# Two token chunks share one Strassen down projection in a transformer block

## The chip, the cores and the metric

The kernel runs on one core of a Trainium2 chip. The metric is the device time of one execution in microseconds. Five engines work side by side: TensorE (PE) multiplies matrices, VectorE (DVE) and ScalarE (ACT) work element by element, GpSimd (POOL) issues some of the transfers and does a few sums, SyncE (SP) issues most transfers. A matmul here is one instruction that multiplies a 128x128 tile by a 128x512 tile and adds the product to a bank of 128x512 fp32 sums in PSUM, of which there are eight.

## The reference

One transformer block on 2048 tokens of width 1024, in bf16: a norm, a sliding attention of 32 heads in which every token looks at 8 tokens (itself and every second one before it), and a gated feed forward without a nonlinearity.

```python
x = A_x                                             # (1, 2048, 1024)
qkv = layernorm(x) @ wqkv                           # wqkv 1024 x 3072
idx = pos[:, None] - 2 * arange(8)[None, :]         # 8 keys a token, masked where idx < 0
logits = einsum("bhsd,bhswd->bhsw", q, k[idx]) * 32 ** -0.5
o = einsum("bhsw,bhswd->bhsd", softmax(logits), v[idx])
h = x + o @ wo                                      # wo 1024 x 1024
n = layernorm(h)
g, u = n @ w_gate, n @ w_up                         # 1024 x 3584 each
out = h + (g * u) @ w_down                          # w_down 3584 x 1024
```

## The kernel before

The tokens are cut into four chunks of 512 (0 to 3). TensorE's instructions stand in this order: q, k and v of all chunks; then for chunk 0 wo and norm, gate and up; wo of chunk 1; down of chunk 0; gate and up of chunk 1; then, interleaved, down of chunk 1 and wo of chunks 2 and 3; at the end chunks 2 and 3 together (the "pair stage": gate, up and down, all in Strassen's way, untouched by the change). Attention is VectorE's work and needs no matmul: it is a generator that hands out a piece at a time. The `Background` object issues such a piece after a group of matmuls, as long as its account of VectorE's time (`rate`, `credit`, `spend`) allows.

```python
    def attention(c):
        qD, kD = qkv_in["q", c], qkv_in["k", c]
        ...
            for j in range(2):
                nc.vector.tensor_tensor(prod[:, j], qD[:], kD[:, :, o:o + SUB], ALU.mult)   # 128x4096
                yield 2.3
        ...
        nc.vector.tensor_tensor(lg[:], lg[:], mx[...], ALU.subtract)
        nc.scalar.activation(lg[:], lg[:], ACTF.Exp, scale=float(DH) ** -0.5)
        yield 3.5
        ...
        nc.gpsimd.dma_start(od[c].rearrange("c g d s -> (c g) d s"), oD[:])
        oT = att.tile([128, KO, 4, SUB], BF, tag="oT", name=f"oT{c}")
        for cp in range(4):
            nc.gpsimd.dma_start(oT[:, :, cp, :], od[c][cp].rearrange(...))
```

The attention's result oD goes to DRAM and comes back transposed as oT, four slices, one for each 128 tokens. `wo_ln2` multiplies oT by wo, adds to the residual h and normalizes on VectorE:

```python
    def wo_ln2(c):
        for t in range(4):
            for hf in range(2):
                ...                                    # 8 matmuls
                nc.vector.tensor_tensor(hs[t][:, bass.ts(hf, 512)], ps[:], hs[t][:, bass.ts(hf, 512)], ALU.add)
                if hf == 1:
                    stats(hs[t], mv4, t)               # two BN_STATS, one aggregate, on VectorE
                    rstd_of(mv4, rs4, t, t + 1)
                elif t > 0:
                    norm(t - 1)
                bg.step(GROUP_US)
```

Gate and up of a chunk, and the down projection of chunk 0:

```python
    def ffn1(c, lnT, at={}):
        for b in range(7):
            for j in range(4):
                mm_group(pg, wts["wg", c, b], j, lnT)          # 8 matmuls
                nc.scalar.copy(gs[:], pg[:])
                bg.step(GROUP_US)
                mm_group(pu, wts["wu", c, b], j, lnT)          # 8 matmuls
                nc.scalar.copy(us[:], pu[:])
                nc.vector.tensor_tensor(gs[:], gs[:], us[:], ALU.mult)
                abs_sum(c, b, j)                               # ScalarE: sum of |w|, 128x1024
                bg.step(GROUP_US)
    def ffn2(c, hf, hT, hs, between={}):
        for b in range(4):
            for j in range(7):
                for t in range(4):
                    nc.tensor.matmul(acc[t][:], lhsT=hT[f][:, bass.ts(t, 128)], rhs=wts["wd", c, hf, b][:, j, :], ...)
                abs_sum_down(hf, b, j)                         # ScalarE: sum of |w|, 128x512
```

The sums of absolute values fix powers of two by which weights and h are scaled before they become fp16, the type in which Strassen's sums and differences are formed (`scale_gu` for gate and up, `scale_d` for down, `scale_h1` for h).

Chunk 1's down projection is one level of Strassen (in Winograd's form): seven products of half-sized blocks in place of eight. The four blocks of h are two halves of the tokens (256 each) by even and odd tiles of the inner dimension, those of w_down even and odd tiles by halves of the columns. `dprod` is one such product for 128 tokens (14 matmuls), and each runs for q = 0 and 1:

```python
    def dprod(ps, q, lhs, rhs, fresh, lo=0, n=TC):
        for k in range(NP):                                    # 14
            nc.tensor.matmul(ps[...], lhsT=lhs[k][:, bass.ts(q, 128)], rhs=rhs[k][...], ...)
    hT = ffn1(1, lnT2, {0: scale_d.rows, 2: scale_d.total, (6, 1): first_blocks})
    E1 = {"11": [t[:, 0:256] for t in hT[0::2]], "21": [t[:, 256:512] for t in hT[0::2]],
          "12": [t[:, 0:256] for t in hT[1::2]], "22": [t[:, 256:512] for t in hT[1::2]]}
```

Of the kernel before, what the change touches and what calls it, by code (L numbers as in the profile page):

```python
# [18 lines left out]
D = 1024  # L19
# [59 lines left out]
def kernel(  # L79
# [41 lines left out]

    bg = Background()
# [13 lines left out]
    def stream_wd(c, hf):  # L136
        for b in range(4):
            stream.append((("wd", c, hf, b), wd_v[:, bass.ts(b, 7), bass.ts(hf, 512)], 7))

    NH = NF // 4  # L140
    for c in range(2):
        stream_wo(c)
        if c > 0:
            stream_wd(0, 0)
            stream_wd(0, 1)
        for b in range(7):
            stream.append((("wg", c, b), wg_v[:, :, bass.ts(b, 512)], KO))
            stream.append((("wu", c, b), wu_v[:, :, bass.ts(b, 512)], KO))
    def stream_down(name, e, hf, halves):
        for a in halves:  # L150
            stream.append((("dn", name, a), wd_e[e][:, bass.ts(a, 7), bass.ts(hf, 512)], 7))

    stream_down("21", 1, 0, (0, 1))
    stream_down("11", 0, 0, (0, 1))
    stream_wo(2)
    stream_down("12", 0, 1, (0,))
# [100 lines left out]
    class NormOnScalar(Norm1):  # L257

        def sums(self):
            room = small.tile([128, 4, 4], F32, tag="nroom", name=f"nroom{self.c}")  # L260
            self.s, self.nm, self.ss, self.nb = (room[:, i, :] for i in range(4))
            junk = lnp.tile([128, D], BF, tag="ln", name=f"njunk{self.c}")
            xs = xtiles[self.c]
            for t in range(4):
                nc.scalar.activation(junk[:], xs[t][:], ACTF.Copy, accum_out=self.s[:, t:t + 1])
                yield "later", GROUP_US
            nc.scalar.activation(self.nm, self.s, ACTF.Copy, scale=-1.0 / D)
            for t in range(4):
                nc.scalar.activation(junk[:], xs[t][:], ACTF.Square, bias=self.nm[:, t:t + 1],
                                     accum_out=self.ss[:, t:t + 1])  # L270
                yield "later", GROUP_US
            nc.scalar.activation(self.rs4[:], self.ss, ACTF.Ln, bias=eps[:], scale=1.0 / D)
            nc.scalar.activation(self.rs4[:], self.rs4[:], ACTF.Exp, scale=-0.5)
            for t in range(4):
                nc.scalar.activation(self.nb[:, t:t + 1], self.nm[:, t:t + 1], ACTF.Copy, scale=self.rs4[:, t:t + 1])

        def rows(self):
            for t in range(4):
                ln = lnp.tile([128, D], BF, tag="ln", name=f"ln{self.c}_{t}")
                nc.scalar.activation(ln[:], xtiles[self.c][t][:], ACTF.Identity, bias=self.nb[:, t:t + 1],  # L280
                                     scale=self.rs4[:, t:t + 1])
                self.lns[t] = ln
                self.transpose(t)
                yield "later", GROUP_US
# [158 lines left out]

    def attention(c):
        qD, kD = qkv_in["q", c], qkv_in["k", c]
        lg = att.tile([128, W, SUB], F32, tag="lg", name=f"lg{c}")
        for wp in range(W // 2):
# [14 lines left out]
            yield 1.0  # L462
        if c == 0:
# [6 lines left out]
        nc.vector.tensor_tensor(lg[:], lg[:], mx[:, None, :].to_broadcast((128, W, SUB)), ALU.subtract)  # L470
        nc.scalar.activation(lg[:], lg[:], ACTF.Exp, scale=float(DH) ** -0.5)
# [9 lines left out]
        prefetch_qk(c + 1)  # L481
# [7 lines left out]
        for wp in range(W // 2):  # L489
# [7 lines left out]
            prefetch_qk(c + 1)  # L497
# [12 lines left out]
        oTs[c] = oT  # L510
        while c + 1 < NCH and ("q", c + 1) not in qkv_in:
# [7 lines left out]
    def wo_ln2(c):  # L519
# [8 lines left out]
        for t in range(4):  # L528
            for hf in range(2):
# [12 lines left out]
                bg.spend(0.7)  # L542
                bg.step(GROUP_US)
        norm(3)
        retire(2)
        return lnT, hs
# [35 lines left out]
    scale_gu, scale_d, scale_h = Scale("gu", 56), Scale("d", 56), Scale("h", 56)  # L582
    scale_h1 = Scale("h1", 28)

    def abs_sum(c, b, j):
        wt = wts["wg" if c == 0 else "wu", c, b]
        junk = lnp.tile([128, 2, 512], BF, tag="ln", name=f"junk{c}_{b}_{j}")
        scale_gu.add(28 * c + 4 * b + j, wt[:, bass.ts(j, 2), :], junk[:])

    def abs_sum_down(hf, b, j):  # L590
        junk = lnp.tile([128, 512], BF, tag="ln", name=f"junkd{hf}_{b}_{j}")
        scale_d.add(28 * hf + 7 * b + j, wts["wd", 0, hf, b][:, j, :], junk[:])
# [5 lines left out]
    def abs_sum_h1(f, ht):  # L598
        junk = lnp.tile([128, TC], BF, tag="ln", name=f"junke{f}")
        scale_h1.add(f, ht[:], junk[:])  # L600

    def ffn1(c, lnT, at={}):
        hT = []
        for b in range(7):
            if b == 5 and c + 1 < NCH:
                hss[c + 1] = load_x(c + 1, "h", nc.sync)
            for j in range(4):
                pg = psum.tile([128, TC], F32, tag="mm", name=f"pg{c}_{b}_{j}")
                mm_group(pg, wts["wg", c, b], j, lnT)
                gs = t1k.tile([128, TC], BF, tag="t1k", name=f"gs{c}_{b}_{j}")  # L610
                nc.scalar.copy(gs[:], pg[:])  # L611
                bg.step(GROUP_US)
                pu = psum.tile([128, TC], F32, tag="mm", name=f"pu{c}_{b}_{j}")
                mm_group(pu, wts["wu", c, b], j, lnT)
                us = t1k.tile([128, TC], BF, tag="t1k", name=f"us{c}_{b}_{j}")
                nc.scalar.copy(us[:], pu[:])  # L616
                nc.vector.tensor_tensor(gs[:], gs[:], us[:], ALU.mult)  # L617
                abs_sum(c, b, j)
                bg.spend(0.45)
                bg.step(GROUP_US)  # L620
                hT.append(gs)
                if (b, j) in at:
                    at[b, j]()
                f = len(hT) - 3
                if c == 1 and f >= 0:
                    abs_sum_h1(f, hT[f])
# [3 lines left out]
        if c == 1:  # L630
            for f in range(NF - 2, NF):
                abs_sum_h1(f, hT[f])
        return hT

    def ffn2_store(c, t, hf, acc, hs, lo=0, n=512):
        cols = bass.ds(hf * 512 + lo, n)
        nc.vector.tensor_tensor(hs[t][:, cols], acc[:], hs[t][:, cols], ALU.add)
        nc.sync.dma_start(outf[bass.ds(c * TC + t * 128, 128), cols], hs[t][:, cols])

    def ffn2(c, hf, hT, hs, between={}):  # L640
        acc = [psum.tile([128, 512], F32, tag="mm", name=f"acc{c}_{hf}_{t}") for t in range(4)]
        for b in range(4):
            for j in range(7):
                f = b * 7 + j
                for t in range(4):
                    nc.tensor.matmul(acc[t][:], lhsT=hT[f][:, bass.ts(t, 128)],  # L646
                                     rhs=wts["wd", c, hf, b][:, j, :],
                                     start=(f == 0), stop=(f == NF - 1))
                if c == 0:
                    abs_sum_down(hf, b, j)  # L650
                bg.step(0.86)
            retire()
            if b in between:
                between[b]()
        for t in range(4):
            ffn2_store(c, t, hf, acc[t], hs)
            bg.spend(0.7)


# [95 lines left out]
    pump(6)  # L755
    bg.add(norm1[3].sums(), bg.now + 18.0)
    start_attention(0)
    qkv(1, range(4))
# [11 lines left out]
    bg.rate = 0.98  # L770
# [3 lines left out]
    lnT2, hs = nxt  # L774
    hT = ffn1(0, lnT2)
    bg.finish(atts[1])
    nxt = wo_ln2(1)
    for hf in range(2):
        ffn2(0, hf, hT, hs)
    lnT2, hs = nxt  # L780
# [37 lines left out]
    dn = {}  # L818

    def first_blocks():  # L820
        dn["11"] = [wts["dn", "11", a] for a in range(2)]
        dn["21"] = [wts["dn", "21", a] for a in range(2)]
        conv_down(dn["11"])

    hT = ffn1(1, lnT2, {0: scale_d.rows, 2: scale_d.total, (6, 1): first_blocks})
    hs1 = hs
    E1 = {"11": [t[:, 0:256] for t in hT[0::2]], "21": [t[:, 256:512] for t in hT[0::2]],
          "12": [t[:, 0:256] for t in hT[1::2]], "22": [t[:, 256:512] for t in hT[1::2]]}
    EF = {k: [f16(a) for a in E1[k]] for k in E1}
    conv_down(dn["21"], nc.scalar)  # L830
    scale_gu.rows()
    scale_h1.rows()
    bg.finish(atts[2])
    ex = [psum.tile([128, TC], F32, tag="mm", name=f"ex{q}") for q in range(2)]
    ey = [psum.tile([128, TC], F32, tag="mm", name=f"ey{q}") for q in range(2)]
    for q in range(2):
        dprod(ex[q], q, E1["11"], fcells(dn["11"]), True)
        bg.step(3.0)

    h3 = att.tile([128, 4, D], BF, tag="qD", name="h3")  # L840
    nc.sync.dma_start(h3[:], x[bass.ts(3, TC), :].rearrange("(t p) d -> p t d", p=128))
    hss[3] = [h3[:, t, :] for t in range(4)]
# [3 lines left out]
    def wo_adds(c, at):  # L846
        hs = hss[c]
        for t in range(4):
            for hf in range(2):
# [5 lines left out]
                bg.spend(0.7)  # L855
                bg.step(GROUP_US)
# [133 lines left out]
    for t in range(4):  # L990
        ln_rows(3, t, l3)
# [166 lines left out]
```

## Time and profile before

| what | value |
|---|---|
| time, median of 3 runs | 777.28 us (776.94 to 777.30) |
| span of the profiled run | 775.2 us |
| granted TensorE clock | 1.000 |
| matmuls in the trace | 3691 |
| ScalarE busy | 484.0 us (62% of the span) |
| GpSimd busy | 142.1 us (18%) |
| wo of chunk 1 begins | 287.88 us |
| down of chunk 0 | 301.69 to 350.0 us |
| first matmul of the pair stage | 516.77 us |

Times of the profile are microseconds from the start of the span. A group of instructions is named by line, engine, operation and "output<-input" with the shapes, then comes the number of instructions, then busy time and mean duration in ns, then the idle time of the engine just before them with what ended it. The chain of waits follows the end of the program back, at each step to what released it. A row of the table by stage gives each engine's busy time within a stretch. Since a matmul's end is modelled, busy time of PE is not proof of work at full rate; the chain and the waits are.

### The profile page before, as it was taken

What the parts mean: (1) busy time and instruction counts of PE and PEld (TensorE: products, weight loads), DVE (VectorE), ACT (ScalarE), POOL (GpSimd) and SP (SyncE); (2) the same over time, 40 slices, a digit from 0 to 9 for tenths busy, and PEclk for the clock granted to TensorE, in tenths of its full rate; (3) what the DMA queues carried; (4) which work ended last, traced back from release to release, by engine and by line L of the source; (5) the groups of instructions that cost most, each with busy time, mean ns of one, the idle gap of its engine ahead of it and who ended that gap; (6) DMA issues with size and microseconds to landing.
All of it is one profiled execution on the core that took longest, in us unless ns stands there. A gap on an engine that the chain in (4) does not pass through costs nothing.

```text
span 775.2 us, 10420 instructions
## 1 busy us (share of the span) xinstructions
PE 769.3 (99%) x3691; PEld 353.5 (46%) x3691; DVE 605.3 (78%) x766; ACT 484.0 (62%) x1040; POOL 142.1 (18%) x152
## 2 busy tenths in 40 slices
PE   8999999999999999999999999999999999999998
PEld 6444444444444444444444444444444444444444
DVE  5639999999999989999979859985553444578863
ACT  4639564322866662965777899746677776788240
POOL 0000000200002000011000001008778687600000
PEclk9999999999999999999999999999999999999999
DMA  8998896997947964978445592644332423740001
GB/s 278 265 260 199 157 230 151 299 271 224 310 133 236 308 235 125 288 257 277 142 143 192 182 299 68 157 98 114 109 95 69 109 59 106 240 140 28 0 28 55
DMA packets 183716, 134.38 MB, mean 173 GB/s; under 512 B 81264, under 2 KB 176496, under 8 KB 181616
## 3 DMA queue, kind: packets, MB, share of 16 engines
q1 hardware_dynamic: 176912, 110.12, 50.9%
q0 software_dynamic: 3584, 22.02, 8.9%
q10 hardware_dynamic: 3168, 1.57, 0.8%
q8 instruction: 29, 0.48, 0.3%
q14 instruction: 23, 0.19, 0.1%
HBM read 104.86 MB, written 22.02 MB: 164 GB/s over the span
## 4 chain that ended last, share of the span: by engine, by line
PE 93%; DVE 3%; DMA 2%; ACT 1%; issue 0%; ACTq 0%; DVEq 0%
PE ps L411 20%; PE pg L411 12%; PE pu L411 12%; PE dx L807 6%; PE pz L700 6%; PE acc L646 6%; PE py L700 6%; PE px L700 6%; PE wo L532 4%; PE wo L852 4%; PE pv L700 3%; PE dy L807 3%; PE ex L807 2%; DMA lnT<-lnr 1%; DMA w_qkv<-in_A_wqkv_dram 1%; PE ps L372 1%
## 5 line engine op out<-in xcount | busy, mean ns | idle before, releaser
L411 PE MATMUL ps<-lnT,w_qkv 128*128 128x512 bf16 x736 | 159.5, 379 | 0.0
L411 PEld LDWEIGHTS <-w_qkv 128*128 128x128 bf16 x736 | 71.9, 98 | 86.2
L411 PE MATMUL pu<-lnT,w_wu 128*128 128x512 bf16 x448 | 105.8, 379 | 0.0
L411 PE MATMUL pg<-lnT,w_wg 128*128 128x512 bf16 x448 | 105.8, 379 | 0.0
L324 ACT CAST sg<-ps 128x512 bf16<-128x512 f32 x96 | 55.2, 585 | 52.3 <-PE ps L411 49.2
L451 DVE TENSOR_TENSOR prod<-qD,kD 128x4096 bf16<-128x4096 bf16 x32 | 72.4, 2285 | 12.8 <-DMA kD<-kd 12.7
L494 DVE TENSOR_TENSOR pv<-vD,at 128x4096 bf16<-128x4096 bf16 x32 | 72.5, 2285 | 0.3
L700 PEld LDWEIGHTS <-sw 128*128 128x128 f16 x448 | 43.8, 98 | 53.8 <-issue 1.2
L411 PEld LDWEIGHTS <-w_wu 128*128 128x128 bf16 x448 | 43.8, 98 | 52.9
L411 PEld LDWEIGHTS <-w_wg 128*128 128x128 bf16 x448 | 43.7, 98 | 52.8
L616 ACT CAST us<-pu 128x512 bf16<-128x512 f32 x56 | 33.0, 590 | 43.0 <-PE pu L411 41.8
L700 PE MATMUL px<-lnT,ws 128*128 128x512 bf16 x224 | 55.2, 379 | 0.0
L700 PEld LDWEIGHTS <-ws 128*128 128x128 f16 x336 | 32.9, 98 | 39.7
L506 POOL DMA_DIRECT2D od<-oD x4 | 2.2, 542 | 264.3 <-DVE oD L504 264.3
L646 PE MATMUL acc<-w_wd,gs 128*128 128x512 bf16 x224 | 48.5, 379 | 0.0
L681 POOL TENSOR_TENSOR sw<-ws 128x512 f16<-128x512 f16 x26 | 30.0, 1152 | 85.1 <-PE py L700 77.8
L611 ACT CAST gs<-pg 128x512 bf16<-128x512 f32 x56 | 32.6, 583 | 12.9 <-PE pg L411 10.6
L453 DVE TENSOR_TENSOR prod<-prod 128x4096 bf16<-128x4096 bf16 x16 | 36.6, 2289 | 0.4
L560 ACT ACTIVATE junkd<-w_wd 128x512 bf16<-128x512 bf16 x56 | 34.3, 613 | 0.0
L646 PEld LDWEIGHTS <-gs 128*128 128x128 bf16 x224 | 21.9, 98 | 26.4
L617 DVE TENSOR_TENSOR gs<-gs,us 128x512 bf16<-128x512 bf16 x56 | 23.5, 419 | 12.5 <-ACT us L616 12.5
L185 ACT ACTIVATE rs<-mv,eps 128x1 f32<-128x1 f32 (+1 forms) x21 | 6.2, 297 | 42.0 <-DVE mv L182 36.6
(321 smaller groups left out, 1391.5 us busy)
## 6 DMA issues: line engine op xcount, KB each, us to landing
w_wg<-in_B_w_gate_dram SPq DMA_DIRECT2D x14, 1024.0 KB, 6.7
w_wu<-in_B_w_up_dram SPq DMA_DIRECT2D x14, 1024.0 KB, 5.4
w_wd<-in_B_w_down_dram SPq DMA_DIRECT2D x8, 896.0 KB, 6.2
w_pair<-in_B_w_gate_dram SPq DMA_DIRECT2D x14, 512.0 KB, 4.0
w_pair<-in_B_w_up_dram SPq DMA_DIRECT2D x14, 512.0 KB, 5.2
w_wo<-in_A_wo_dram SPq DMA_DIRECT2D x6, 1024.0 KB, 6.2
w_qkv<-in_A_wqkv_dram SPq DMA_DIRECT2D x5, 1024.0 KB, 11.0
kd<-sg SPq DMA_DIRECT2D x32, 144.0 KB, 3.3
```

Source lines behind the costliest of these rows:

```text
L324: nc.scalar.copy(sg[:, HB:HB + TC], ps[:])
L411: nc.tensor.matmul(ps[:], lhsT=wt[:, ko, bass.ts(j, 128)], rhs=rhs[:, ko, :], start=(ko == 0), stop=(ko == KO - 1))
L451: nc.vector.tensor_tensor(prod[:, j], qD[:], kD[:, :, o:o + SUB], ALU.mult)
L453: nc.vector.tensor_tensor(prod[:, :, 0:16], prod[:, :, 0:16], prod[:, :, 16:32], ALU.add)
L494: nc.vector.tensor_tensor(pv[:, j], vD[:, :, o:o + SUB], at[:, w, None, :].to_broadcast((128, DH, SUB)), ALU.mult)
L532: nc.tensor.matmul(ps[:], lhsT=oTs[c][:, kk, t, :], rhs=wts["wo", c, hf][:, kk, :], start=(kk == 0), stop=(kk == KO - 1))
L560: nc.scalar.activation(junk, src, ACTF.Abs, accum_out=self.l1[:, k:k + 1])
L611: nc.scalar.copy(gs[:], pg[:])
L616: nc.scalar.copy(us[:], pu[:])
L646: nc.tensor.matmul(acc[t][:], lhsT=hT[f][:, bass.ts(t, 128)], rhs=wts["wd", c, hf, b][:, j, :], start=(f == 0), stop=(f == NF - 1))
L700: nc.tensor.matmul(ps[:], lhsT=lhs[:, ko, :], rhs=rhs[:, ko, :], start=(fresh and ko == 0), stop=(ko == 3), skip_group_check=not fresh)
L807: nc.tensor.matmul(ps[:, bass.ds(lo, n)], lhsT=lhs[k][:, bass.ts(q, 128)], rhs=rhs[k][:, bass.ds(lo, n)], start=(fresh and k == 0), stop=( ...
```

## The change

The down projections of chunks 0 and 1 become one Strassen product: the rows of the left matrix are now the two chunks, so block A11 is chunk 0's even tiles of h, A12 its odd ones, A21 and A22 those of chunk 1, and each of the seven products runs for four row tiles of 128 tokens. It is meant to save matmuls: chunk 0's down projection was a standard one.

```diff
-    for hf in range(2):
-        ffn2(0, hf, hT, hs)
-    hT = ffn1(1, lnT2, {0: scale_d.rows, 2: scale_d.total, (6, 1): first_blocks})
-    for q in range(2):
-        dprod(ex[q], q, E1["11"], fcells(dn["11"]), True)
+    hT0 = ffn1_first(nxt[0], {(4, 2): wo_1})
+    bg.finish(norm2[1])
+    ffn1_second(norm2[0].lnT, {})
...
+    for q in range(4):
+        dprod(xs[q], q, A11, cells_of(b11, NH), True)
...
+    for q in range(4):
+        dprod(xs[q], q, A12, cells_of(b21, NH), False)
+        put(0, q, 0, hs0[q][:, 0:512], xs[q], 1.0, hs0[q][:, 0:512])
```

What stands around it has to change with it.

*Storage.* h of chunk 0 stays in SBUF (28 tiles), so h of chunk 1 no longer fits; it is made in a ring of three places, stored in DRAM and read back in blocks. Half of chunk 0's and all of chunk 1's residual rows go to DRAM and back, too.

```diff
+            nc.vector.tensor_tensor(g, g, u, ALU.mult)                 # 128x1024, two tiles of h at a time
+            nc.sync.dma_start(hd1[:, bass.ts(i, 2), :], g)
...
+    load_h1(a21, 0)
+    load_h1(a22, 1)                                                    # a22 is read a second time later
```

*wo of chunk 1* moves into the middle of chunk 0's gate and up (block 4, j = 2), and its norm goes to ScalarE, one step after each group of matmuls:

```diff
+    class Norm2(NormOnScalar):
+        pace = 0.9 * GROUP_US
+        def finish(self):
+            yield from self.devs()
+            yield from self.rows()
...
+    def wo_1():
+        bg.finish(sums)
+        bg.finish(atts[1])
+        n = wo_norm(1)
+        norm2.append(n.finish())
+        bg.add(norm2[1], bg.now, first=True)
```

*Sums of absolute values.* Gate and up are summed four row tiles at a time (128x2048), the gate's blocks 4 and 5 during chunk 1; of w_down, one half of the columns is read through a ring buffer during the q, k, v stage, the other half is summed from the Strassen blocks B11 and B21.

```diff
-        scale_gu.add(28 * c + 4 * b + j, wt[:, bass.ts(j, 2), :], junk[:])
+        scale_gu.add((14 if key == "wu" else 0) + 2 * b + i, wt[:, bass.ts(i, 4), :], junk)
+                if j % 2 and b not in (4, 5):
+                    abs_sum("wg", 0, b, j // 2, junk[:])
+    def abs_down():
+        for p in range(7):
+            scale_d.add(p, rows_of(p), rows_of(p))
+            if p + 2 < 7:
+                load(p + 2)
+            yield "later", 4.9 * GROUP_US
```

*The attention's place in the order.* A later attention waits until the one before has ended, the exp is issued a step later, chunk 3's q and k are loaded one step later, and the account of VectorE's time changes:

```diff
+        while c and c - 1 not in over:
+            yield "later", 1.0
+        yield "later", 4.0 if c == 0 else 1.5
         nc.scalar.activation(lg[:], lg[:], ACTF.Exp, scale=float(DH) ** -0.5)
-            prefetch_qk(c + 1)
+            if c != 2 or wp > 0:
+                prefetch_qk(c + 1)
-    bg.rate = 0.98
+    bg.rate = 1.03
+    bg.spend(8.0)
```

*The order of the products.* With B the blocks of w_down, S and T the sums of Strassen's form (S1 = A21 + A22, S2 = S1 - A11, S3 = A11 - A21 formed as A22 - S2, S4 = A12 - S2; T1 = B12 - B11, T2 = B22 - T1, T3 = B22 - B12, T4 = B21 - T2): wo of chunk 2, A11·B11, A12·B21, S1·T1, S2·T2, S4·B22, wo of chunk 3, S3·T3, A22·T4, then the pair stage as before. Each result is scaled back, added to the residual rows and stored by `put`.

## The prediction

> **What bounds the kernel now.** I read the page's busy line first, then the chain of waits, then TensorE's waits, and last a table of busy time by stage. The page says which engine has no room:
>
> ```profile
> PE 769.3 (99%) x3691; PEld 353.5 (46%) x3691; DVE 605.3 (78%) x766; ACT 484.0 (62%) x1040; POOL 142.1 (18%) x152
> PE 93%; DVE 3%; DMA 2%; ACT 1%; issue 0%; ACTq 0%; DVEq 0%
> ```
>
> Busy PE is modelled, so 99% alone proves little. The chain proves it: from 27 us to the pair stage its long pieces are all matmuls.
>
> ```profile
> 27.16 136.41 PE ps L411 x632
> 163.56 13.81 PE wo L532 x64
> ...
> 287.88 13.81 PE wo L532 x64
> 301.69 48.35 PE acc L646 x224
> 446.76 6.04 PE ex L807 x28
> 456.50 10.36 PE wo L852 x48
> ```
>
> Two things are read here. 48.35 us / 224 = 0.2159 us for one 128x512 matmul, back to back: the price of a matmul. And each piece starts where the one before ended: 287.88 + 13.81 = 301.69. Then TensorE's waits. Past 27 us there are two, both behind the last output additions of chunk 1:
>
> ```profile
> 519.08 1.02 PE L700 MATMUL pv<-prodx,sw 128*128 128x512 f16 x4 [0.41 <-DVE h L812]
> ...
> 521.19 1.02 PE L700 MATMUL pv<-prodx,sw 128*128 128x512 f16 x4 [0.22 <-DVE h L812]
> ```
>
> Together 0.63 us. So nothing can be gained but by fewer matmuls, by those 0.63 us, or in the first 27 us, which the change leaves alone. The stage table says who would take over (columns: window, then busy us of PE, PEld, DVE, ACT, POOL, each with its instructions; clock; DMA share; GB/s):
>
> ```profile
> 191.20:253.00 61.80, 61.80 (x288) 28.00 (x287) 60.19 (x50) 40.98 (x78) 4.62 (x6) 1.00 0.77 232
> 253.00:302.00 49.00, 49.00 (x229) 22.21 (x228) 45.17 (x56) 25.34 (x48) 1.07 (x2) 1.00 0.72 242
> 302.00:350.00 48.00, 48.00 (x224) 21.77 (x223) 46.85 (x33) 35.30 (x116) 3.12 (x4) 1.00 0.78 243
> 350.00:399.00 49.00, 49.00 (x230) 22.23 (x228) 43.40 (x53) 34.24 (x72) 1.51 (x3) 1.00 0.58 185
> 399.00:447.00 48.00, 48.00 (x224) 21.71 (x223) 43.72 (x36) 39.46 (x90) 0.56 (x1) 1.00 0.55 185
> ...
> 479.00:493.00 14.00, 14.00 (x66) 6.37 (x65) 14.00 (x38) 11.62 (x22) 0.00 (x0) 1.00 0.04 12
> ```
>
> VectorE is 89 to 100% busy in each of these. It is idle 22% of the span, but not in the stages that the change rewrites: 239.3 of 255.8 us from 191.2 to 447.
>
> **What the Trainium skill says.** "TensorE: Matmul & The Clock Gate", section "Wait — 56ns, not 53.3ns?", puts back-to-back 512-column matmuls at 215.7 ns start to start on a warm array; the trace's 215.9 agrees, and the clock is 1.00 in every row above. "VectorE: DVE Perf Modes", section "Why `tensor_tensor` can't do 2×_2P or 4×": two source tensors use up both read ports. That fits these rows: the sum of two tensors costs nearly twice the scaling of one of the same size.
>
> ```profile
> L494 DVE TENSOR_TENSOR pv<-vD,at 128x4096 bf16<-128x4096 bf16 x32 | 72.5, 2285 | 0.3
> L617 DVE TENSOR_TENSOR gs<-gs,us 128x512 bf16<-128x512 bf16 x56 | 23.5, 419 | 12.5 <-ACT us L616 12.5
> L800 DVE TENSOR_TENSOR kx<-w_dn,w_dn 128x3584 f16<-128x3584 f16 x2 | 4.0, 2014 | 0.0
> L788 DVE TENSOR_SCALAR w_dn<-w_dn,sbd 128x3584 f16<-128x3584 bf16 x3 | 3.4, 1148 | 0.2 <-issue 0.2
> ```
>
> "ScalarE: Activation LUTs", section "What ACT_TABLE_LOAD costs", gives an ACTIVATE with immediates 186 ns + 0.833 ns an element. For the new 2048-element sums this makes 1.89 us, an estimate; the 1024-element sums of before show 1067 ns, where the same formula gives 1039. "DMA: Bandwidth & Descriptors", section "Issuing engines are not separate DMA queues": loads issued by different engines share the same 16 DMA engines. The DMA shares of 0.55 to 0.78 above are therefore what the new reloads find occupied.
>
> **The change part by part.**
>
> *Matmuls.* Before, chunk 0's down projection is standard: 4 row tiles x 28 x 2 halves = 224. Chunk 1 has its own seven products: 7 x 2 x 14 = 196. After: one set of seven for both chunks, 7 x 4 x 14 = 392. 420 - 392 = 28 matmuls less; 28 x 0.2159 = 6.04 us. The projections, gate and up, wo, and chunks 2 and 3 keep theirs. TensorE without new waits gives 777.28 - 6.04 = 771.24, and 770.6 if the 0.63 us go as well. This is the floor.
>
> *The new timetable of TensorE*, in groups of 8 matmuls (1.73 us) from 191.2: gate and up of chunk 0 until blocks 0 to 3 and half of block 4 are done (36 groups: 253.35), wo of chunk 1 to 267.2 (before, from 287.88), the rest to 301.7, gate and up of chunk 1 to 398.4, wo of chunk 2 to 412.2. Then products of 56 matmuls, 12.09 us each: A11·B11 to 424.3, A12·B21 to 436.4, S1·T1 to 448.5, S2·T2 to 460.6, S4·B22 to 472.7; wo of chunk 3 to 486.5; S3·T3 to 498.6; A22·T4 to 510.7, where the pair stage begins (before at 516.77). Every part is judged by what must be ready at these times.
>
> *oT of chunk 1*, needed at 253.35, 34.5 us sooner than before. Before's GpSimd timeline:
>
> ```profile
> 236.17 0.54 POOL L506 DMA_DIRECT2D od<-oD  x1 [62.50 <-DVE oD L504]
> 245.09 3.54 POOL L509 DMA_DIRECT2D oT<-od  x4 [8.39 <-PE pg L411]
> ```
>
> The store took till 245.1 (the 8.39 us; the engine named had long been done), and the median landing of an oT slice is 4.8 us on the page. VectorE's order in front of oD hardly changes: I sum 44.6 us of work from 191.2, so oD is done near 235.9, as before. The first slice lands at 249 to 253 us and each later one is needed 3.45 us (two groups) after it. Cost: 0 to 1 us.
>
> *VectorE until the last gate product of chunk 1.* After's order, at the durations above (4096 elements 2.26 us, 512 elements 0.36, somewhat under the rows' means because neighbours overlap: an estimate): 44.6 us to oD of chunk 1, then 162.1: the rest of attention 2 and the larger part of 3 (some 140), 13 products of 1024 elements 8.2, 16 of 512 5.8, 8 additions of wo 5.0, with the small rest. 191.2 + 44.6 + 162.1 is about 398, and TensorE is at 398.4. No slack, but no deficit: chunk 1's norm went to ScalarE (8 BN of 0.68, 4 of 0.2, 4 rows of 0.55 = 8.4 us less) and the eight additions of chunk 0's output (8 x 0.68 = 5.4) are gone.
>
> *Sums for the pair on VectorE*, from 398: 40 us up to T1 = B12 - B11: rest of attention 3 13.6, wo additions 5, scaling of A21, A22, B11 and B12 about 7, S1 and T1 8, outputs 2.8. T1's second half is ready at 438 to 440; the eighth matmul of S1·T1 reads it first, at 436.4 + 7 x 0.216 = 437.9. Cost 0.3 to 2 us. T2 and S2 (2 x 1.97 + 14 x 0.35) are ready at 447.6 to 449.6 for 448.5: mostly hidden behind the former wait. A22·T4 adds into the banks of S3·T3, so each bank's output must be read first; by the same sum over after's order (additions of wo, statistics of chunk 3, T4, then the outputs) VectorE has read the first at about 499.3 against 498.6: 0.7 us.
>
> *ScalarE.* The row sums of gate and up become 28 of 1.9 us instead of 56 of 1.07 + 0.2, the down sums 23 instead of 56, sums of h grow from 28 to 42. In chunk 1's gate and up, two steps cost 4 x 0.48 + 1.9 + 1.05 = 4.9 us of TensorE's 6.9 (6.8 with an additional gate sum): hidden. The 16 sums over B11 and B21 cost 12 x 1.05 + 4 x 0.61 = 15 us from 403, done at 418.5 to 421; their total is wanted on TensorE at 421.3. No cost, or a few tenths.
>
> *Transfers.* New: h of chunk 1 out (14 x 256 KB) and A21, A22 and again A22 back, residual rows out and in. Those of 398 to 420 (B12's and B21's parts, A21, A22, some 6.4 MB) take 21 us at 300 GB/s, which the page's slices show to be reached: on land by 418 to 420, first needed from 413 to 423. No cost to 1 us.
>
> Sum: 771.24 - 0.63 + about 0.4 (oT) + 0.6 (T1) + 0.7 (output before A22·T4) = 772.3.
>
> **The rivals.** (a) VectorE takes over. For: it is 94% busy over the stretch and my sum ends on the very microsecond of TensorE's. Each exp also makes it wait for ScalarE, 1 to 3 us an attention, unless the added yield fills that. Against: the same engine carried 60.19 of 61.80 us in before without a single TensorE wait there. It would show as waits of 2 to 5 us before S1·T1 and S2·T2: 774 to 777. (b) A transfer is late: oT of chunk 1, A21 and A22, or wo of chunk 0, whose buffer now comes later because a ring for the down sums takes one. For: shares of 0.8 and landings of 8.2 us for one megabyte. Against: the median 4.8. 774 to 778. (c) Everything is hidden: 770.6 to 771.3. The order was plainly laid out against these deadlines (later q and k of chunk 3, wo of chunk 1 split from its norm), so I give (c) and my sum together 70%, (a) 20%, (b) 10%.
>
> **Range and chances.** Predicted 772.3. Low 770.4 is the floor less the spread of runs (0.36 us); high 775.5 holds the middle of (a). More than 2% faster would be below 761.7, which 28 matmuls can't give; more than 2% slower is above 792.8, which needs 22 us of new waits. Chances 0.01, 0.97, 0.02.
>
> **What would show it.** Right: TensorE 28 matmuls fewer; the pair stage beginning at 510.7 plus the waits; waits under 2 us, named after VectorE's T1 or an output. Wrong: a wait in front of wo of chunk 1 (oT step), in gate and up of chunk 1 (VectorE or buffers), at A11·B11 (transfers, total), or a tail after the pair stage's start longer than 258.4 us. The prediction fails if such waits sum above 4 us.

## The result and the profile after

| | before | after |
|---|---|---|
| time, median | 777.11 us (4 runs, 776.74 to 777.30) | 774.48 us (4 runs, 773.42 to 775.07) |
| ratio after to before, 95% interval | | 0.9965, 0.9948 to 0.9982 |
| span of the profiled run | 775.2 us | 772.1 us |
| matmuls in the trace | 3691 | 3663 |
| wo of chunk 1 begins | 287.88 us | 253.38 us |
| first matmul of the pair stage | 516.77 us | 514.63 us |

The changed kernel is 2.6 us faster. 5.0 were predicted, 6.0 are what the matmuls left out are worth. The page of the changed kernel, busy line and shares of the chain by engine:

```profile
PE 764.2 (99%) x3663; PEld 351.1 (45%) x3663; DVE 606.2 (79%) x718; ACT 513.4 (66%) x979; POOL 141.9 (18%) x152
PE 75%; DVE 15%; ACT 4%; issue 3%; DMA 3%; ACTq 0%; DVEq 0%; SPq 0%
```

28 matmuls are gone, as counted. The second line is new: before, 93% of the chain was TensorE; now VectorE carries 15%. That reads like a kernel bound by VectorE for 15% of its time, but it means something else: the chain is followed back from the end, and where it meets a wait of TensorE it steps to whoever ended that wait and walks back along that engine as long as it stays busy. One wait suffices to hand over a hundred microseconds. TensorE's timeline from A11·B11 to the pair stage has that wait (the bracket is idle time, and its releaser):

```profile
412.38 9.23 PE L944 MATMUL ex<-w_dn,gs 128*128 128x512 bf16 x42
424.49 0.38 PE L645 MATMUL ey<-rowbd,ones 128*128 128x512 bf16 x1 [2.88 <-DVE rowbd L640]
424.70 3.18 PE L944 MATMUL ex<-w_dn,gs 128*128 128x512 bf16 x14
428.07 12.25 PE L944 MATMUL ex<-w_dn,gs 128*128 128x512 bf16 x56 [0.18 <-ACT ey L1067]
440.15 12.25 PE L944 MATMUL ev<-w_dn,a 128*128 128x512 f16 x56
...
502.54 12.25 PE L944 MATMUL ez<-t,a22r 128*128 128x512 f16 x56
514.63 1.67 PE L826 MATMUL px<-lnT,ws 128*128 128x512 bf16 x7
```

Only these two waits of over 0.1 us stand in the whole span after the start. The single matmul `ey<-rowbd,ones` sums the absolute values of w_down over the partitions (the "total"); TensorE waits for `rowbd`, the row sums reduced on VectorE. Then A12·B21 waits for ScalarE's copy of ex. The brackets count from the modelled ends; from the starts they cost more: 42 matmuls from 412.38 end at 421.45, so 3.04 us at the total, and 424.70 + 14 x 0.2159 = 427.72, so 0.35 us at A12·B21. Together 3.39 us. Why `rowbd` was late stands in VectorE's timeline:

```profile
417.12 1.27 DVE L925 TENSOR_SCALAR a<-a,sbh 128x4096 f16<-128x4096 bf16 x1
420.55 1.29 DVE L925 TENSOR_SCALAR a<-a,sbh 128x4096 f16<-128x4096 bf16 x1 [2.16 <-DMA a<-hd]
421.87 2.29 DVE L1042 TENSOR_TENSOR a<-a,a 128x4096 f16<-128x4096 f16 x1
424.08 0.17 DVE L639 TENSOR_REDUCE rowd<-l1d 128x1 f32<-128x23 f32 x1
424.28 0.16 DVE L640 CAST rowbd<-rowd 128x1 bf16<-128x1 f32 x1
424.35 2.28 DVE L534 TENSOR_TENSOR oD<-oD,pv 128x4096 bf16<-128x4096 bf16 x1
```

In order: A21 scaled, a wait of 2.16 us for A22 from DRAM, A22 scaled, S1's first half, and only then the reduction, although ScalarE had ended its last sum at 418.8. And A22 came late in a full stretch. This is the share of DMA engines (in tenths) and the rate in 40 slices of 403 to 422 us:

```profile
DMA  0999899999999999999999999999999999997100
GB/s 4 323 280 259 241 237 336 351 354 367 364 369 369 358 351 347 377 328 332 347 341 351 347 354 343 356 347 347 349 347 349 343 349 345 354 347 220 39 22 24
```

And the view of A21's and A22's tiles gives the landing times of their four loads:

```profile
DMA to landing us min/median/max: 11.0/12.4/12.9
```

The transfers run without a gap from 403.5 to 420 us, from 406 us on at some 350 GB/s. B12's 1.8 MB were issued first and A21's 1.8 MB next. The load of A22's first megabyte was issued at 407.67, as soon as SyncE had finished issuing A21's second load (407.62), and took 12.9 us: it landed at 420.5. A22's second part landed at 422.7.

The stages before it, for comparison with the same windows of before: TensorE full in all of them.

```profile
191.20:253.00 61.80, 61.80 (x289) 27.96 (x286) 59.43 (x50) 45.81 (x84) 4.63 (x6) 1.00 0.82 249
...
302.00:350.00 48.00, 48.00 (x224) 21.80 (x223) 47.66 (x31) 36.04 (x60) 4.63 (x6) 1.00 0.70 224
350.00:399.00 49.00, 49.00 (x229) 22.21 (x228) 46.55 (x40) 43.18 (x66) 0.00 (x0) 1.00 0.72 241
```

VectorE stands at 59.4 of 61.8, 47.7 of 48 and 46.6 of 49 us.

**The balance**, by starts of matmuls. Before's two waits at the pair stage are gone; by starts they had cost 519.08 - 516.77 - 8 x 0.2159 = 0.58 and 521.19 - 519.94 - 4 x 0.2159 = 0.39 us, in sum 0.97 and not the 0.63 of the brackets. The totals of the scales cost 0.37 us more: before, those of gate and up and of w_down were matmuls of 64 columns and took 0.03 us each, that of h had 512 columns and took 0.22; now all three have 512 columns and take 0.22, 0.22 and 0.21. And the total of h starts 0.09 us late, at 406.98 instead of 404.73 + 10 x 0.2159 = 406.89. So 6.04 + 0.97 - 3.39 - 0.37 - 0.09 = 3.16 us; the spans differ by 3.1.

### The profile page after: what moved, and what is told of

Its sections match the earlier page's. It is cut to its first block, busy times and chain, and to the rows that moved or that the text cites. A ratio compares the mean times of both kernels' runs of the same rounds, so it can differ in the third digit from the quotient of the medians.

```text
span 772.1 us, 10299 instructions
## 1 busy us (share of the span) xinstructions
PE 764.2 (99%) x3663; PEld 351.1 (45%) x3663; DVE 606.2 (79%) x718; ACT 513.4 (66%) x979; POOL 141.9 (18%) x152
## 4 chain that ended last, share of the span: by engine, by line
PE 75%; DVE 15%; ACT 4%; issue 3%; DMA 3%; ACTq 0%; DVEq 0%; SPq 0%
PE ps L431 21%; PE dx L944 6%; PE py L826 6%; PE px L826 6%; PE pz L826 6%; PE pu L431 4%; PE pg L431 4%; PE pv L826 3%; PE ez L944 3%; PE ey L944 3%; DVE pv L523 3%; PE dy L944 3%; DVE prod L477 2%; PE wo L998 2%; PE wo L602 2%
## 5 line engine op out<-in xcount | busy, mean ns | idle before, releaser
L431 PE MATMUL pg<-lnT,w_wg 128*128 128x512 bf16 x224 | 52.9, 379 | 0.0
L431 PE MATMUL pu<-lnT,w_wu 128*128 128x512 bf16 x224 | 52.9, 379 | 0.0
L431 PE MATMUL pwu<-lnT,w_wu 128*128 128x512 bf16 x224 | 52.9, 379 | 0.0
L431 PE MATMUL pwg<-lnT,w_wg 128*128 128x512 bf16 x224 | 52.9, 379 | 0.0
L807 POOL TENSOR_TENSOR sw<-ws 128x512 f16<-128x512 f16 x26 | 30.0, 1155 | 85.5 <-PE pv L826 51.9
L944 PEld LDWEIGHTS <-gs 128*128 128x128 f16 (+1 forms) x280 | 27.4, 98 | 36.4 <-issue 3.6
L843 ACT COPY py<-px 128x512 f32<-128x512 f32 x28 | 16.0, 570 | 27.8 <-PE px L826 27.8
L808 POOL TENSOR_TENSOR sw<-sw,ws 128x512 f16<-128x512 f16 x26 | 30.0, 1155 | 2.0
L810 POOL TENSOR_TENSOR sw<-ws,sw 128x512 f16<-128x512 f16 x26 | 30.0, 1155 | 0.0
L809 POOL TENSOR_TENSOR sw<-ws 128x512 f16<-128x512 f16 x26 | 30.0, 1155 | 0.0
```

The source lines that it names most:

```text
L431: nc.tensor.matmul(ps[:], lhsT=wt[:, ko, bass.ts(j, 128)], rhs=rhs[:, ko, :], start=(ko == 0), stop=(ko == KO - 1))
L807: eng.tensor_tensor(sw[:, i, 0], a21, a22, ALU.add)
L808: eng.tensor_tensor(sw[:, i, 1], sw[:, i, 0], a11, ALU.subtract)
L809: eng.tensor_tensor(sw[:, i, 2], a11, a21, ALU.subtract)
L810: eng.tensor_tensor(sw[:, i, 3], a12, sw[:, i, 1], ALU.subtract)
L843: nc.scalar.copy(yb[i][:], xb[i][:])
```

## The experiments

Theory 1, from this reading: transfers at their full rate delay A22, VectorE stands still for it with the reduction behind it, and as VectorE has no slack, all its later work shifts. The rivals: the place of the reduction in VectorE's queue alone is the cause; or A22's buffer comes free late.

**The changed kernel again**, beside the next three kernels.

> The changed kernel again, for comparison within one session. Both theories: 773.4 to 775.1 us, TensorE waits about 2.9 us at the total of the down scale near 424.5 us.

774.93 us (773.27 to 775.57, 5 runs; the kernel before, beside it, 777.09). Ratio 0.9967 (0.9954 to 0.9979). The wait is there, 2.67 us. In its executions the span is 771.5 or 771.8 us where the granted clock is 1.000, and 772.9 to 773.2 where it is 0.997 or 0.998; the next run explains it. One of the four executions of the first measurement had 773.2 us at a listed clock of 1.000, which stays unexplained.

**The reduction ahead of A22.**

```diff
             conv_h1(a21, 0)
+            scale_d.rows()
             conv_h1(a22, 0)
             s1_half(0)
-            scale_d.rows()
```

> Only the reduction of the down sums is put ahead of the scaling of A22 on VectorE. Theory 1 (the wait for A22 delays all of VectorE, and the total is only the first to show it): the wait at the total falls from 2.9 to under 0.5 us, but T1 is no earlier (first half near 439.0, second near 441.5), so a new wait of about 3 us appears at the start of S1·T1; time within 0.5 us of the changed kernel. Rival (the reduction's place is the cause): the 3.4 us are gained, time near 771.1.

774.87 us (773.40 to 775.88, 8 runs), 0.997 (0.9959 to 0.998): nothing gained, at the full clock neither (spans of 771.6). TensorE's, VectorE's and ScalarE's timelines of this kernel:

```profile
421.48 0.38 PE L645 MATMUL ey<-rowbd,ones 128*128 128x512 bf16 x1
421.69 3.19 PE L944 MATMUL ex<-w_dn,gs 128*128 128x512 bf16 x14
427.50 3.11 PE L944 MATMUL ex<-w_dn,gs 128*128 128x512 bf16 x9 [2.62 <-ACT ey L1067]
```

```profile
420.25 1.29 DVE L925 TENSOR_SCALAR a<-a,sbh 128x4096 f16<-128x4096 bf16 x1 [1.03 <-DMA a<-hd]
421.57 2.29 DVE L1042 TENSOR_TENSOR a<-a,a 128x4096 f16<-128x4096 f16 x1
423.78 2.28 DVE L534 TENSOR_TENSOR oD<-oD,pv 128x4096 bf16<-128x4096 bf16 x1
425.99 0.15 DVE L647 COPY totd<-ey 128x1 f32<-128x1 f32 x1
```

```profile
426.79 2.39 ACT L1067 ACTIVATE ey<-ex,sbd 128x512 f32<-128x512 f32 x4 [1.52 <-DVE ibd L654]
```

The total comes without a wait, and A12·B21 starts at 427.50 instead of 428.07 (427.78 in the changed kernel again). So the rival falls, and so does part of mine: I had put the new wait at T1. The next gate is nearer. A12·B21 adds into the banks of A11·B11, and these have to be copied by ScalarE first, scaled with a number that VectorE forms from the total in five small operations; and those stand in VectorE's queue behind S1 and a piece of attention (`oD`). They follow A22 as before: A22's scaling began at 420.25 here, at 420.55 and 420.25 in the two profiles of the changed kernel.

The table by stretch of this run shows a second thing (the last three columns are clock, DMA share, GB/s):

```profile
427.40:429.00 1.60, 1.50 (x6) 0.63 (x6) 1.60 (x1) 1.60 (x4) 0.00 (x0) 0.83 0.32 104
429.00:431.00 2.00, 1.78 (x5) 0.76 (x5) 1.82 (x2) 2.00 (x5) 0.00 (x0) 0.50 0.00 0
431.00:433.00 2.00, 2.00 (x8) 0.79 (x7) 0.59 (x1) 2.00 (x4) 0.00 (x0) 0.79 0.50 131
```

After an idle time of 427.50 - 421.69 - 14 x 0.2159 = 2.79 us the granted clock fell to one half, about 1 us after TensorE had started again. The three rows give its length: 2 x (1 - 0.83) x 1.6 + 2.0 + 2 x (1 - 0.79) x 2.0 = 3.4 us, until about 432 us. The Trainium skill, "TensorE: Matmul & The Clock Gate", section "Part 1: The HAM clock gate (the "warmup" mystery)", says that the array falls to half rate after an idle window of about 3.4 us, counted by a free-running window; the half rate is seen here, and an idle time of 2.8 us was enough. From 427.50 to 441.27 the 56 matmuls of A12·B21 took 13.77 us instead of 12.09, half of 3.4 us more. That fits the difference of about 1.5 us between the executions of the changed kernel with and without the full clock, and the spread of its runs over 2.3 us where those of before spread over 0.9.

**A21 and A22 loaded ahead of B12.**

```diff
-    load_down(b12, 0, 1)
...
-    load_h1(a21, 0)
-    load_h1(a22, 1)
+    load_h1(a21, 0, parts=(0,))
+    load_h1(a22, 1, parts=(0,))
+    load_h1(a21, 0, parts=(1,))
+    load_h1(a22, 1, parts=(1,))
+    load_down(b12, 0, 1)
```

> Only the order of loads changes: A21 and A22 ahead of B12. Theory 1 (A22 is late because the transfers of 403 to 421 run at the full rate of the 16 engines and B12's 1.8 MB go first): A22's first part lands by 416, VectorE's wait of 2.2 us goes, the total's wait falls to 0.5 to 1.0 us, time about 2.3 us less than the changed kernel. Rival (the buffer of A22 comes free late): A22 lands at 419 to 421 all the same, time unchanged.

771.61 us (771.37 to 772.01, 5 runs), 0.9928 (0.9916 to 0.9941): 3.3 us less than the changed kernel beside it. VectorE's and then TensorE's timeline of it:

```profile
416.99 2.47 DVE L925 TENSOR_SCALAR a<-a,sbh 128x4096 f16<-128x4096 bf16 x2
419.49 2.29 DVE L1044 TENSOR_TENSOR a<-a,a 128x4096 f16<-128x4096 f16 x1
421.70 0.17 DVE L639 TENSOR_REDUCE rowd<-l1d 128x1 f32<-128x23 f32 x1
```

```profile
422.12 0.38 PE L645 MATMUL ey<-rowbd,ones 128*128 128x512 bf16 x1 [0.64 <-DVE rowbd L640]
422.33 3.18 PE L944 MATMUL ex<-w_dn,gs 128*128 128x512 bf16 x14
425.70 12.25 PE L944 MATMUL ex<-w_dn,gs 128*128 128x512 bf16 x55 [0.18 <-ACT ey L1069]
```

Both blocks are scaled back to back (one line, x2). The first megabyte of A21 and of A22, in the changed kernel and here (the last figure is the median time to landing):

```profile
a<-hd SPq DMA_DIRECT2D x2, 1024.0 KB, 11.9
a<-hd SPq DMA_DIRECT2D x2, 1024.0 KB, 6.6
```

A22's first load starts at 404.87 instead of 407.67 and takes 7.2 us instead of 12.9, so it lands at 412.1 instead of 420.5. The same 5.8 MB move in the same stretch; only the order differs. So it was what stood ahead of A22 in the queue, not its buffer. The edit moves two things, B12 behind and A22's first part ahead of A21's second; how much each of them gives was not separated. The waits left are 0.80 and 0.35 us by starts, too short for the clock to fall: it is 1.000 in all five executions. The gain has two parts, then: 2.0 us of waits (by starts 2.83 + 0.35 in the changed kernel run beside it, 1.15 here), and the 1.5 us or so of half clock in those executions that had it. The spans at full clock agree: 769.5 to 769.8 against 771.5 and 771.8.

**Both edits.**

> Both edits. Theory 1: no wait at the total, up to 1 us at T1; time 2.3 to 3.0 us less than the changed kernel. If the reduction's place alone were the cause: no better than that edit alone.

772.28 us (772.10 to 772.77, 5 runs), 0.9938 (0.9924 to 0.9951): 0.7 us more than the load order alone. The total no longer waits, but A12·B21 does, 1.56 us, for ScalarE's copy. With the reduction early, VectorE waits 0.44 us for ScalarE's last sum before it, and S1, `oD` and the five operations come 0.6 us later: the last of them starts at 425.40 instead of 424.81 and A12·B21 at 426.29 instead of 425.70. What counts is when the chain ends, not when its first link is ready.

**The three edits.** Theory 2, then: the gate is the chain from the total through the scale's operations to ScalarE's copy. In addition one piece of attention 3 goes from ahead of the scale's operations to after S1·T1, so that `oD` (2.3 us) no longer stands in front of them.

```diff
         if q == 1:
-            pull(1)
             conv_h1(a21, 1, nc.scalar)
...
-    pull(2)
+    pull(3)
     retire(4)
```

> The new load order, the reduction ahead of A22's scaling, and one piece of attention 3 (2.3 us of VectorE) moved from ahead of the scale's small operations to after S1·T1. Theory 2 (what TensorE waits for is the chain total, scale, copy of ex on ScalarE, and on VectorE that chain stood behind S1 and the attention piece): no wait over 0.3 us from 412 us to the pair stage; time 770.3 to 770.9 us. Rival (T1 or the attention's end becomes the bound): a wait of 1 to 3 us at S1·T1 or at wo of chunk 3; time 772 to 774.

> The three edits again. Theory 2: 770.3 to 771.1 us, 0.5 to 1.0 us below the new load order alone (771.6), spans of 768.5 to 769.4 us; no TensorE wait from 412 us to the pair stage.

First time 770.90 us (770.37 to 774.84, 6 runs), 0.9926 (0.9911 to 0.9941); second time 770.83 (770.74 to 771.51, 4 runs), 0.9918 (0.9904 to 0.9933). TensorE now runs from A11·B11 through A12·B21 in one piece:

```profile
422.19 15.46 PE L944 MATMUL ex<-w_dn,gs 128*128 128x512 bf16 x69
437.49 12.25 PE L944 MATMUL ev<-w_dn,a 128*128 128x512 f16 x56
```

This is the fastest version, 6.3 and 6.5 us below the kernel before. 777.2 - 6.04 - 0.97 + 0.37 = 770.56 is what is left if nothing waits. The new load order with the moved piece alone, without the early reduction, was not run. One of the ten executions took 774.84 us, at a clock of 0.997; no trace shows that one, and its cause is open.

**The price of 28 matmuls**, in the kernel before. Seven of 28 inner tiles of one half of chunk 0's down projection are left out, so that half of the output is incomplete.

```diff
                 for t in range(4):
+                    if hf == 1 and 7 <= f < 14:
+                        continue
                     nc.tensor.matmul(acc[t][:], lhsT=hT[f][:, bass.ts(t, 128)],
```

> The kernel before, with 28 of the 224 matmuls of chunk 0's down projection left out (seven of the 28 inner tiles in one half; the output of that half lacks them), all else kept. Price as predicted: 6.04 us less than before, near 771.05. If TensorE were held by another engine there, the gain would be under 4 us.

771.56 us (771.46 to 771.69, 4 runs), 0.9927 (0.9914 to 0.994): 5.64 us less. The missing 0.4 us are found at the start of the pair stage, where before had 0.41 and 0.22:

```profile
513.48 1.02 PE L702 MATMUL pv<-prodx,sw 128*128 128x512 f16 x4 [0.86 <-DVE h L814]
515.59 1.02 PE L702 MATMUL pv<-prodx,sw 128*128 128x512 f16 x4 [0.23 <-DVE h L814]
```

So the 6.04 us hold, and TensorE was the bound; 0.46 us of them come back as a longer wait for VectorE's output additions, which don't move up with it.

**Three parts of the change undone**, each in the kernel with the new load order (771.6), where the clock stays full. Chunk 3's q and k as early as before:

```diff
-        if c != 2:
-            prefetch_qk(c + 1)
+        prefetch_qk(c + 1)
...
-            if c != 2 or wp > 0:
-                prefetch_qk(c + 1)
+            prefetch_qk(c + 1)
```

> The kernel with the new load order, but chunk 3's q and k loaded as early as in the kernel before. If the later load protects gate and up's weights (transfers are 98% busy from 267 to 302 us): new TensorE waits of 1 to 3 us before 302 us. If it only tidies: within 0.3 us of the kernel with the new load order (771.6).

771.62 us (771.39 to 771.68, 5 runs), no new wait: it only tidies. The norm of chunk 1 allowed two steps after one group:

```diff
-        pace = 0.9 * GROUP_US
+        pace = 0.4 * GROUP_US
```

> The kernel with the new load order, but the norm of chunk 1 on ScalarE may put two steps after one group of matmuls (pace 0.4 groups in place of 0.9). VectorE-has-no-slack theory: ScalarE's copies come later in bursts, a gate product on VectorE waits up to 2.5 us more near 280 us, and that shows as a TensorE wait only after 405 us: 772.5 to 774. Rival (banks and VectorE cover the bursts): within 0.3 us of 771.6.

771.59 us (771.54 to 772.00, 4 runs): no difference. VectorE's waits are those of the kernel it is made from (1.55 us near 284), so the pace is not what spaces the steps there; what does was not tried.

All gate sums in chunk 0:

```diff
-                if j % 2 and b not in (4, 5):
+                if j % 2:
...
-                        elif b in (4, 5):
-                            abs_sum("wg", 1, b, j // 2, junk)
```

> The kernel with the new load order, but all gate sums in chunk 0 (four sums of 1.9 us more on ScalarE between 268 and 300 us, where it is busy 30 of 35 us beside the norm of chunk 1). If they had to move: TensorE waits for PSUM copies or for chunk 1's normalized rows, 1 to 3 us. If the eight banks cover it: within 0.3 us of 771.6.

776.41 us (775.88 to 777.71, 21 runs), 0.9992 (0.9985 to 0.9998): 4.8 us slower than its base, more than either side expected, and in another place. No PSUM copy and no row of the norm held TensorE. VectorE waits for an exp on ScalarE, and TensorE waits 114 us later, for the row sums of h (`rowbh`):

```profile
297.19 0.69 DVE L502 TENSOR_TENSOR trs<-lg 128x512 f32<-128x512 f32 x1 [2.90 <-ACT lg L499]
```

```profile
411.06 0.61 PE L645 MATMUL l1psh<-rowbh,ones 128*128 128x512 bf16 x1 [4.18 <-DVE rowbh L640]
```

In the base, the kernel with the new load order, the same exp costs VectorE 0.79 us, and gate products (gate times up, on VectorE) wait 1.5 us in all between 280 and 291, against 0.98 + 2.52 + 0.74 here. That is 4.8 us more, and VectorE's last gate product ends 4.2 us later. `rowbh` had no slack: in the changed kernel VectorE finished it at 406.92, and TensorE's matmul follows at 406.98, as close behind it as where it did wait (here 411.01 and 411.06).

The exp issued at once:

```diff
-        yield "later", 4.0 if c == 0 else 1.5
         nc.scalar.activation(lg[:], lg[:], ACTF.Exp, scale=float(DH) ** -0.5)
```

> The kernel with the new load order, but the attention's exp issued at once as in the kernel before, so that it stands in ScalarE's queue ahead of copies that could go first. VectorE-has-no-slack theory: the exp comes somewhat sooner for VectorE but ScalarE idles in front of it by 1 to 3 us and the gate products wait for copies; net change of VectorE's waits under 1 us, time within 1 us of 771.6. Rival (the added step is what keeps VectorE fed): VectorE waits 2 us more at each of three exps, time 774 to 777.

775.43 us (774.75 to 776.29, 11 runs), 0.9974 (0.9965 to 0.9983): 3.8 us slower. The time lies in the rival's range, but not for its reason: VectorE's own waits between 200 and 411 us grow only from 4.6 to 6.0 us. But with a step less the attention's pieces move forward in the order, and one more stands ahead of the last gate product. Its timeline, and below it that of the base:

```profile
403.06 2.29 DVE L533 TENSOR_TENSOR oD<-oD,pv 128x4096 bf16<-128x4096 bf16 x1
405.27 0.69 DVE L748 TENSOR_TENSOR ring<-ring 128x1024 bf16<-128x1024 bf16 x1
```

```profile
401.81 0.68 DVE L749 TENSOR_TENSOR ring<-ring 128x1024 bf16<-128x1024 bf16 x1
402.41 0.68 DVE L1002 TENSOR_TENSOR h<-wo,h 128x512 bf16<-128x512 f32 x1
403.01 2.28 DVE L534 TENSOR_TENSOR oD<-oD,pv 128x4096 bf16<-128x4096 bf16 x1
```

2.3 us of attention and 1.4 us of waits make 3.7, near the 3.5 us by which the product is late, and TensorE waits 3.23 us for `rowbh`. In both undone parts the idle time exceeds 3 us, and the clock is below 1.000 in all but one of 32 executions.

## Why the prediction was right, and where it was not

The time, 774.48 us, lies in the predicted range. The gain, 2.6 us, is about half of the 5.0 forecast. The matmuls and the floor were right; the waits were not: those that the sum holds did not come, and one that it put at nothing did. That the time falls into the range is luck in part: its upper end had been set for rival (a). Of the signs named for a wrong prediction one appeared, a wait at A11·B11 for the total, but its 3.39 us stay under the 4 that were named as the limit.

- *Matmuls*: right. 28 fewer, and their price of 6.04 us confirmed by leaving 28 out of the kernel before. That the 0.63 us at the pair stage would go was right; they were worth 0.97, since the brackets count from modelled ends.
- *oT of chunk 1*: in place. The store was issued at 237.39, the slices from 244.23, and wo began at 253.38 without a wait. The 0.4 us set aside were not needed.
- *VectorE until the last gate product*: the sum was right, but it held no idle time. Predicted 398, measured 402.6 us; the trace has 6.6 us of waits ahead of it (on exps, PSUM copies and one transfer). I had named 1 to 3 us an exp in the rivals and not added them. That it cost TensorE no more than 0.09 us was luck: the next use, `rowbh`, came just at its turn.
- *T1*: ready at 441.6 instead of 438 to 440, no wait, as TensorE was late itself. In the fastest version it is ready at 438.9, with S1·T1 from 437.49, and there is none either. *Output before A22·T4*: no wait. Together 1.3 us set aside in vain.
- *ScalarE*: right. Its 16 sums over B11 and B21 ran from 403.78 to 418.8, as predicted (15 us), and a 2048-element sum took 1.9 to 2.0 us, where the estimate was 1.89. That the totals became wider, 0.37 us on TensorE, was left out.
- *Transfers*: here the prediction failed. "On land by 418 to 420, first needed from 413 to 423. No cost to 1 us." They landed by 422.7, A22's first part by 420.5, not far from what was worked out; but I compared one time of landing with a span of needs and did not place each block in VectorE's queue. A22 was needed at 418.4, with B12 and A21 issued ahead of it; VectorE stopped for 2.16 us; and the reduction for the total and the scale's operations stood behind it. That also undid "their total is wanted on TensorE at 421.3. No cost, or a few tenths": the sums were in time, their reduction was not. These two terms, put at up to 1 us and at a few tenths, and at nothing in the sum, came to 3.39 us, in three of five executions with some 1.5 us of half clock on top. With 1.7 us of waits that did not come, 772.3 - 1.7 + 3.39 + 0.37 + 0.09 - (0.97 - 0.63) = 774.1 us.
- *The rivals*: what happened is (b), a late transfer of A22, which I gave 10% and which reached TensorE through (a), a VectorE without slack. Kept apart as rivals, they looked less likely than they are as one chain.

## What to carry to other kernels

Where a second engine is busy nearly all the time beside the bound one (here 95 to 99% in the three stages shown), place every wait of that engine in its queue, in order: each microsecond it stands still goes on to whatever it does later, and can surface as a wait of the bound engine a hundred microseconds on, under the name of an operation that is not to blame. When several transfers start together at the full rate, give their order the order of first use; it moves no byte less and was worth 3.3 us here. Before moving the operation that a wait is named after, follow the chain to the gate behind it: with the total early, TensorE only waited at the next one.

## What the runs showed of the hardware that was not expected

TensorE's clock fell to 0.50 for 3.4 us after an idle time of 2.8 us in the middle of dense work, at a cost of about 1.5 us, in six of eight executions of one kernel. In the changed kernel, with 2.8 us in the second profile and 3.0 in the first, the clock was below 1.000 in three of five executions of the second measurement, in none of four of the first, and in neither of the profiled ones. After 1.7 us (426.29 - 421.55 - 14 x 0.2159 in the kernel with both edits) it fell in none of five. In this kernel a wait of about 3 us can thus cost 4.5, and not in every run.
